# The gate side of the last feed-forward group as seven half products among the output products, with row sums and projections by DMA

## The chip, the cores and the metric

One core of a Trainium2 chip runs the whole program. The metric is the device time of one execution in microseconds (us). Matmuls run on TensorE (PE in the profile, its weight loads PEld), elementwise work on VectorE (DVE), activations and copies out of PSUM on ScalarE (ACT). GpSimd (POOL) issues the accumulating DMAs and SyncE (SP) most of the others. Every engine works through its own instruction queue in order.

## The reference, cut to what matters

The input x has 2048 tokens of 512 features. After a layer norm, two branches are added to x: a state-space layer with 512 complex states, and a gated feed-forward with 1792 hidden features.

```python
xn = layernorm(x)
Bu = xn @ B_bar.T                      # complex, 512 states
h[t] = Lam_bar * h[t-1] + Bu[t]        # over 2048 tokens
A = 2 * real(h @ C.T) + xn * Dskip
gate, up = xn @ w1, xn @ w3            # 512 -> 1792
B = (silu(gate) * up) @ w2             # 1792 -> 512
out = x + A + B                        # bfloat16
```

## The kernel before, in words

**Tiling.** The tokens go in 4 blocks of 512, a block in 4 chunks of 128, two chunks in a *pair*: 8 pairs, 0 to 7, two for each block. Hidden features go in 14 tiles of 128. For each block the normalised input is transposed (`xnT`), projected to the states (`bu`, or `bu_fast` for blocks 2 and 3), multiplied by a table, scanned over time on VectorE (L505) and multiplied by the table again; the feed-forward writes `silu(gate) * up` next to the states in one tile `act`. The output of a pair is one product of `act` with the stacked weights `w2` and C, 22 tiles deep.

**Seven products for eight.** A product of 2 x 2 quarters is made by seven products of quarters and sums of them. The left quarters are a11, a12, a21, a22, with the row sums s1 = a21 + a22, s2 = s1 - a11 (or, in `row_sums`, the same up to the order: s3 = a11 - a21, s2 = s3 - a22), s4 = a12 - s2 or a12 + s2; the right quarters and their sums t1 to t4 likewise. Three things are made so:

- the output of a pair (`y_fast`, L1036): seven products of 11 matmuls, 256 columns wide (`mms`, L1052). Products are numbered 1 to 7; in pairs 4 to 6 their order is 1, 4, 2, 6, 5, 7, 3 (`ORDER`). In pairs 4 and 5 the third product is put off into the next pair, behind its fifth (`LATER`).
- the projection of blocks 2 and 3 (`bu_fast`, L760): half products of 4 matmuls, 256 columns wide. Partial results are copied between PSUM tiles by ScalarE (L785), and two quarters of each half are finished by an addition of PSUM and a saved sum s5 on VectorE (L792).
- the up side of 12 of the 14 hidden tiles of block 3, in three groups n of four tiles (`glu_last`, L838, `product`, L866). The half products come in the order one, five, two, six, seven, three, four. The gate side of the same tiles (`side`, L845) is plain: 4 matmuls of 512 columns for a tile, read by ScalarE's silu (L860).

**Row sums.** `row_sums` (L992) gives for each pair the tasks for s3 and s2 (VectorE subtractions, L1000, 1408 elements for each partition) and s1 (an accumulating DMA from POOL, L1007, or VectorE).

**What sets the order.** The schedule is by hand: instructions stand on each queue in the order in which Python emits them. `bg`, a `Filler` (L23), holds VectorE's background tasks (table products, scans, row sums) with an estimated cost. `bg.fill()` emits tasks while VectorE's estimated time is not too far ahead of TensorE's; `bg.own` books the time of what is emitted directly; `bg.flush(key)` emits all up to a task of that name. A task with a `ready` that says no holds up the queue behind it. `ssm_tasks` (L462) gives the table products (`pre_a`, `pre_b`), their sum (`pre_c`, by VectorE for block 0 and half 0 of block 2, else by DMA), the scans, and the products after the scan (`post_a` to `post_c`). `seeds` (L1013) puts part of the result into four PSUM tiles ahead of a pair.

**The end of the program.** Pairs 2 and 3 run with block 3's projection between their products. Then comes `glu_last(3)`: tiles 12 and 13 plain, then groups 0, 1 and 2. Then pairs 4 and 5 (block 2), 6 and 7 (block 3). VectorE's scans of block 3 run between.

Of the kernel before, what the change touches and what calls it, by code (L numbers as in the profile page):

```python
# [22 lines left out]
class Filler:  # L23
# [25 lines left out]
    def fill(self, lead=None):  # L49
# [14 lines left out]
def kernel(  # L64
# [33 lines left out]
    LEAD = 1.7  # L98
    LATER = (4, 5)
    AHEAD = (MID, 8, 1, None)  # L100
# [361 lines left out]
    def ssm_tasks(b, posts_last=False, between=(), middle=(), late=()):  # L462
# [5 lines left out]
        def half(hf):  # L468
# [3 lines left out]
            def pre_a():  # L472
                if b == 0:
                    sin_step((2 * hf + 1, 1))
                    nc.vector.tensor_scalar(out=tabe[:, psl, 2, :], in0=tabe[:, psl, 1, :], scalar1=-1.0,
                                            scalar2=None, op0=ALU.mult)
                st["g"] = u_blk[b, hf]
# [6 lines left out]
                nc.vector.tensor_tensor(out=st["p"][:, :, ::-1, :], in0=st["g"], in1=tabe[:, psl, 2:0:-1, :],  # L484
                                        op=ALU.mult)

            def pre_b():
                nc.vector.tensor_tensor(out=st["g"], in0=st["g"], in1=tabe[:, psl, 0:1, :].to_broadcast(FULL),  # L488
                                        op=ALU.mult)
# [32 lines left out]
            def post_c(csl=slice(0, CPB)):  # L522
# [3 lines left out]
                else:  # L526
                    gp.dma_start(out=a, in_=p16, accum_op=ALU.add)  # L527

            if (b, hf) == (1, 1):
                pre_c.ready = lambda: ("squares", 2, CPB - 1) in sins_done  # L530
# [5 lines left out]

        transfers = (post0[2],) + (() if b == NBLK - 1 else (post1[2],)) + ((pre1[2],) if b > 0 else ()) + ((pre0[2],) if b in (1, 3) else ())

# [221 lines left out]
    def bu_fast(b, hf):  # L760
# [7 lines left out]
        else:  # L768
            u = up.tile([P, 2, 2, TBLK], BF16, name="u")
        s5 = glup.tile([P, 2, TBLK], BF16, name="g16").bitcast(FP32).rearrange("p a t -> p (a t)")  # L770
        if (b, hf) != (3, 1):
# [17 lines left out]

        def add(out, ps):  # L790
            bg.own(0.7)
            nc.vector.tensor_tensor(out=out, in0=parts(ps), in1=parts(s5), op=ALU.add)  # L792
# [33 lines left out]
    def up_sums(b):  # L826
# [8 lines left out]
                for out, x, z, op in ((s1, a21, a22, ALU.add), (s3, a11, a21, ALU.subtract),  # L835
                                      (s2, s1, a11, ALU.subtract))]

    def glu_last(b):  # L838
        xnT = xnT_blk[b]
# [36 lines left out]

        def add(out, ps):
            bg.own(0.7)
            nc.vector.tensor_tensor(out=out, in0=halves(ps), in1=halves(s5), op=ALU.add)

        gates = []
        for f in range(4 * NG, NFT):
            if f % 2 == 0:
                tiles = pair_tiles()
            gate_side(f, tiles[0])
            copy(tiles[1][:, f % 2, :], side(w3_sb, f))
            bg.fill()
            if f % 2 == 0 and gates:
                gates.pop()()
            if f % 2 == 1:  # L890
                gates.append(lambda f=f, tiles=tiles: gate(f - 1, tiles))
        for n in range(NG):
            f0 = 4 * n
            a11, a12, a22, s1n, s2n, s3n, s4n = (v[:, :, n, :] for v in (
                up_quarter(0, 0), up_quarter(1, 0), up_quarter(1, 1), s1, s2, s3, s4))
            g, e = (ps_y.tile([P, TBLK], FP32, name="y_ps") for _ in range(2))
            f, z = (ps_bu.tile([P, TBLK], FP32, name="bu_ps") for _ in range(2))
            upper, lower = pair_tiles(), pair_tiles()
            product(g, a11, b11, True)
            copy(f, g)  # L900
            product(e, s1n, t1, True)
            copy(s5, e)
            gate_side(f0, upper[0])
            bg.fill(0.8)
            gates.pop()()
            product(f, a12, b21, False)
            product(g, s2n, t2, False)
            copy(e, g)
            bg.own(0.42)
            nc.vector.tensor_tensor(out=s4n, in0=a12, in1=s2n, op=ALU.subtract)  # L910
            copy(upper[1][:, :, 0:TH], halves(f))
            gate_side(f0 + 1, upper[0])
            bg.fill()
            product(g, s3n, t3, False)
            copy(z, g)
            add(lower[1][:, :, TH:TBLK], g)
            product(e, s4n, b22, False)
            add(upper[1][:, :, TH:TBLK], e)
            gate_side(f0 + 2, lower[0])
            bg.fill()  # L920
            gate(f0, upper)
            product(z, a22, t4, False)
            copy(lower[1][:, :, 0:TH], halves(z))
# [4 lines left out]
        return gates.pop()  # L928

# [59 lines left out]

    sums = {}  # L990

    def row_sums(n, b, p):  # L992
# [6 lines left out]
        def subtract(out, x, z):  # L999
            return lambda: nc.vector.tensor_tensor(out=out, in0=x, in1=z, op=ALU.subtract)  # L1000

        three = (0.84, subtract(s3, a11, a21), ("sums", n))
        two = (0.84, subtract(s2, s3, a22), ("sums", n))
        if n in (1, 6, 7):
            one = (0.84, lambda: nc.vector.tensor_tensor(out=a21, in0=a21, in1=a22, op=ALU.add), ("sums", n))
        else:
            one = (0.0, lambda: gp.dma_start(out=a21, in_=a22, accum_op=ALU.add), ("sums", n))  # L1007
        return [three, two, one] if n > 5 else [three, one, two]

# [3 lines left out]
    def seeds(n):  # L1013
        b, p = pairs[n]
        bg.flush(("res", b))
        if n in (0, 3, 5, 7):
# [16 lines left out]
    later = {}  # L1033
    ORDER = {4: (1,4,2,6,5,7,3), 5: (1,4,2,6,5,7,3), 6: (1,4,2,6,5,7,3)}

    def y_fast(n, then=(), between=()):  # L1036
# [4 lines left out]
        bg.flush(("difference", b))  # L1041
        if p == 0 and b > 1:
            bg.flush(("scan", b + 1))
        c1 = 2 * p
        v = sums[n]
        res = xn_blk[b]
        g, halves, f, z = seeded[n]
# [31 lines left out]
        def product1():  # L1079
            mms(g, v["a11"], weight(0, D1), True)  # L1080
            copy(f, g)
            if b > 0:
                bg.first(list(then))
            steps()
            bg.fill()

        def product2():
# [4 lines left out]
            if n in (2, 3, 4, 5):  # L1092
                gp.dma_start(out=v["s4"], in_=v["s2"], accum_op=ALU.add)
            else:
# [5 lines left out]
            if n + 1 < len(pairs) and n not in (1, 2, 3) and n - 1 not in LATER:  # L1100
                seeds(n + 1)
            steps()

        def product3():
# [7 lines left out]
            if b > 0:  # L1112
                steps()
            bg.fill(0.5 if n == 1 else None)

        def product4():
            mms(z, v["a22"], tsum[3], False)
            copy(q[2], z)
            steps()
            bg.fill(1.2 if b > 0 and n not in LATER else None)  # L1120

        def product5():
# [4 lines left out]
            if b > 0:  # L1127
                bg.fill(0.5 if n == 3 else None)

        def product6():  # L1130
            mms(g, v["s2"], tsum[1], False)
            add(q0, g, o1[:, D2].bitcast(FP16))
            steps()
            bg.fill()

        def product7():
# [5 lines left out]
            if b == 0:  # L1142
                steps()
                bg.fill()

        products = (product1, product2, product3, product4, product5, product6, product7)
        for i in ((1, 5, 2, 6, 4, 3, 7) if b == 0 else (1, 2, 4, 6, 5, 7, 3) if b == 1 else ORDER.get(n, (1, 4, 2, 6, 5, 7, 3))):
# [8 lines left out]
            if n in LATER:  # L1156
                bg.fill()
            if between:
                for step in between.popleft():
                    step()  # L1160
                    bg.fill()
                if n == 3 and not between:
                    bg.first(up_sums(3))
            if n == 2 and i == 7:
                seeds(3)

# [74 lines left out]
    bg.flush("up")  # L1241
    gate = glu_last(3)
    gate()
    for n in range(4, len(pairs)):
        ahead = row_sums(n + 1, *pairs[n + 1]) if n + 1 < len(pairs) else ()
# [6 lines left out]
        y_fast(n, ahead if n == 4 else ())  # L1252

# [29 lines left out]
```

## Time and profile before

| | us |
|---|---|
| median of 3 runs | 201.09 (201.04 to 201.39) |
| span of the profiled execution, first to last instruction | 199.5 |
| busy in it: PE | 195.6 |
| DVE | 181.8 |
| ACT | 135.0 |
| POOL | 51.5 |

Of the profiled execution the profile gives the span alone. The runs' median is 1.6 us above it. All times in the profile count from the start of the span. A row of the timeline gives start, length, engine, line, operation, output and input tiles, shape, and in brackets the idle time before it with what ended it; rows of equal instructions are merged, and neighbours on an engine can overlap a little. A row of groups gives count, busy time, mean length in ns, and idle time. A row of waits gives who waited for whom, the total in us, how often, and the longest.

### The profile page before, as it was taken

What the parts mean: (1) busy time and instruction counts of PE and PEld (TensorE: products, weight loads), DVE (VectorE), ACT (ScalarE), POOL (GpSimd) and SP (SyncE); (2) the same over time, 40 slices, a digit from 0 to 9 for tenths busy, and PEclk for the clock granted to TensorE, in tenths of its full rate; (3) what the DMA queues carried; (4) which work ended last, traced back from release to release, by engine and by line L of the source; (5) the groups of instructions that cost most, each with busy time, mean ns of one, the idle gap of its engine ahead of it and who ended that gap; (6) DMA issues with size and microseconds to landing.
All of it is one profiled execution on the core that took longest, in us unless ns stands there. A gap on an engine that the chain in (4) does not pass through costs nothing.

```text
span 199.5 us, 3700 instructions
## 1 busy us (share of the span) xinstructions
PE 195.6 (98%) x1401; PEld 130.7 (65%) x1401; DVE 181.8 (91%) x254; ACT 135.0 (68%) x281; POOL 51.5 (26%) x75
## 2 busy tenths in 40 slices
PE   8999999999999999999999999999999999999994
PEld 2774444444444488866555468888566678888893
DVE  3689699999999999989999997999999999999972
ACT  4699897699999996968998684362588783111220
POOL 7180289700411134041202305040021303310000
PEclk9999999999999999999999999999999999999999
DMA  4999996991497054730997455838137732941111
GB/s 138 326 277 200 302 186 124 343 273 23 69 181 141 0 105 82 135 105 0 156 148 119 89 92 98 172 83 132 53 59 129 149 56 52 174 92 36 53 44 40
DMA packets 32258, 25.12 MB, mean 126 GB/s; under 512 B 16240, under 2 KB 29936, under 8 KB 32240
## 3 DMA queue, kind: packets, MB, share of 16 engines
q0 software_dynamic: 6128, 11.38, 33.5%
q1 hardware_dynamic: 25536, 13.21, 26.8%
q10 hardware_dynamic: 576, 0.30, 0.5%
q8 instruction: 11, 0.18, 0.4%
q14 instruction: 7, 0.06, 0.1%
HBM read 7.74 MB, written 2.10 MB: 49 GB/s over the span
## 4 chain that ended last, share of the span: by engine, by line
PE 95%; DMA 2%; SPq 1%; issue 0%; DVE 0%
PE gu_ps L587 34%; PE gu_ps L1054 17%; PE y_ps L1054 10%; PE gu_ps L848 7%; PE bu_ps L1054 7%; PE bu_ps L454 3%; PE y_ps L454 3%; PE y_ps L869 3%; PE y_ps L780 3%; DMA w_sb<-in_B_w_dram 2%; PE gu_ps L619 2%; PE gu_ps L780 2%; PE bu_ps L869 1%; PE bu_ps L780 1%; PE bu_ps L619 1%; SPq L166 0%
## 5 line engine op out<-in xcount | busy, mean ns | idle before, releaser
L587 PE MATMUL gu_ps<-xnT,w_sb 128*128 128x512 bf16 x312 | 69.6, 379 | 0.0
L587 PEld LDWEIGHTS <-w_sb 128*128 128x128 bf16 x312 | 30.5, 98 | 34.2
L1054 PEld LDWEIGHTS <-act 128*128 128x128 f16 x462 | 43.5, 98 | 5.4
L596 ACT ACTIVATE g<-gu_ps 128x512 bf16<-128x512 f32 x41 | 24.8, 606 | 6.0 <-PE gu_ps L587 3.6
L597 ACT ACTIVATE u<-gu_ps 128x512 bf16<-128x512 f32 x41 | 24.8, 606 | 4.5 <-PE gu_ps L587 3.7
L505 DVE TENSOR_TENSOR_SCAN u<-rho,ends,u 128x512 bf16<-128x512 f32 x16 | 20.0, 1270 | 0.0
L527 POOL DMA_DIRECT2D act<-p x7 | 9.2, 1320 | 34.0 <-DVE act L519 22.1
L1054 PE MATMUL gu_ps<-w_sb,act 128*128 128x256 bf16 (+3 forms) x126 | 16.0, 267 | 0.0
L848 PE MATMUL gu_ps<-xnT,w_sb 128*128 128x512 bf16 x64 | 15.9, 379 | 0.0
L604 DVE TENSOR_TENSOR act<-g,u 128x1024 f16<-128x1024 bf16 x21 | 14.2, 679 | 0.4 <-ACT u L597 0.4
L860 ACT ACTIVATE g<-gu_ps 128x512 bf16<-128x512 f32 x14 | 8.4, 599 | 5.4 <-PE gu_ps L848 5.0
L454 PEld LDWEIGHTS <-bt 128*128 128x128 bf16 x64 | 6.3, 98 | 7.5
L1077 ACT ACTIVATE x_blk<-gu_ps 128x256 f32<-128x256 f32 (+1 forms) x9 | 3.3, 368 | 10.6 <-PE gu_ps L1054 10.6
L1054 PE MATMUL bu_ps<-w_sb,act 128*128 128x256 bf16 (+3 forms) x84 | 10.4, 264 | 0.0
L1054 PE MATMUL gu_ps<-ct,act 128*128 128x256 f16 (+1 forms) x72 | 10.4, 267 | 0.0
L848 PEld LDWEIGHTS <-w_sb 128*128 128x128 bf16 x64 | 6.3, 98 | 4.8
L505 DVE TENSOR_TENSOR_SCAN u<-rho,u 128x512 bf16<-128x512 f32 x8 | 9.2, 1206 | 0.0
L1054 PEld LDWEIGHTS <-x_blk 128*128 128x128 f16 x88 | 8.6, 98 | 1.0
L1054 PEld LDWEIGHTS <-tw 128*128 128x128 f16 x88 | 8.6, 98 | 1.0
L513 DVE TENSOR_TENSOR p<-u,tabe 128x2048 f16<-128x2048 bf16 (+1 forms) x8 | 8.7, 1085 | 0.1
L519 DVE TENSOR_TENSOR act<-u,tabe 128x2048 f16<-128x2048 bf16 (+1 forms) x8 | 8.7, 1083 | 0.0
L488 DVE TENSOR_TENSOR u<-u,tabe 128x2048 bf16<-128x2048 bf16 x7 | 8.5, 1219 | 0.1
(203 smaller groups left out, 392.5 us busy)
## 6 DMA issues: line engine op xcount, KB each, us to landing
act<-p POOLq DMA_DIRECT2D x6, 512.0 KB, 6.1
xn<-x_blk POOLq DMA_DIRECT2D x4, 512.0 KB, 5.5
out_dram<-xn SPq DMA_DIRECT2D x15, 128.0 KB, 1.7
w_sb<-in_B_w_dram SPq DMA_DIRECT2D x1, 1792.0 KB, 8.2
act<-act POOLq DMA_DIRECT2D x5, 352.0 KB, 4.6
w_sb<-in_B_w_dram SPq DMA_DIRECT2D x2, 768.0 KB, 6.4
u<-p POOLq DMA_DIRECT2D x3, 512.0 KB, 5.1
w_sb<-in_B_w_dram SPq DMA_DIRECT2D x4, 256.0 KB, 4.9
```

Of the source, the lines that this page charges most:

```text
L454: nc.tensor.matmul(out=ps, lhsT=bt[:, ri, dt, pt * P:(pt + 1) * P], rhs=xnT_blk[b][:, dt, :], start=(dt == 0), stop=(dt == NDT - 1))
L505: nc.vector.tensor_tensor_scan(out=v, data0=rho[:, pt:pt + 1].to_broadcast([P, TBLK]), data1=v, initial=init, op0=ALU.mult, op1=ALU.add)
L513: nc.vector.tensor_tensor(out=by_state(st["p16"][:, csl]), in0=by_chunk(st["g"][:, :, ::-1, tsl]), in1=by_chunk(tabe[:, psl, 2:0:-1, tsl]) ...
L519: nc.vector.tensor_tensor(out=by_state(act_state(b, hf)[:, csl]), in0=by_chunk(st["g"][:, :, :, tsl]), in1=by_chunk(tabe[:, psl, 0:1, tsl] ...
L527: gp.dma_start(out=a, in_=p16, accum_op=ALU.add)
L587: nc.tensor.matmul(out=ps[:, tsl], lhsT=w[:, dt, f * P:(f + 1) * P], rhs=xnT[:, dt, tsl], start=(dt == 0), stop=(dt == NDT - 1))
L596: nc.scalar.activation(out=g16[:, f % 2, :], in_=g_ps, func=ACT.Silu)
L597: nc.scalar.activation(out=u16[:, f % 2, :], in_=u_ps, func=ACT.Copy)
L604: nc.vector.tensor_tensor(out=act_gates(b, f - 1), in0=split(g16), in1=split(u16), op=ALU.mult)
L780: nc.tensor.matmul(out=out[:, h * TH:(h + 1) * TH], lhsT=left[:, h, k, :], rhs=right[:, k, :], start=(start and h == 0 and k == 0), stop=( ...
L848: nc.tensor.matmul(out=ps, lhsT=w[:, dt, f * P:(f + 1) * P], rhs=xnT[:, dt, :], start=(dt == 0), stop=(dt == NDT - 1))
L1054: nc.tensor.matmul(out=out, lhsT=left[:, k, :], rhs=right[k][:, cols], start=(start and k == 0), stop=(k == NK - 1), skip_group_check=True)
```

## The change

1. **Gate side of group 2 by half products.** The four plain gate sides of the third group become seven half products. Their row sums (`gate_sums`) are made by VectorE in the slots of the up sums of groups 0 and 1 that are no longer needed, and in place in `w1`. Where the up side adds into an SBUF tile, the gate side adds in PSUM and then takes the silu.
2. **Third group beside pair 4.** Its up products one and five stay ahead of pair 4; the other twelve steps go in between pair 4's products, after product 1: two and six; after 4: seven, three; after 2: four (`last`), and the gate's one and five; after 6: two, six; after 5: seven, three; after 7: four and a gate multiplication; after 3: the last gate multiplication. Pair 4's third product is no longer put off (`LATER` holds 5 alone); pair 5's seeds use other PSUM tiles, and come after pair 4's product 7.
3. **VectorE's queue in pairs 4 and 5.** `bg.fill` does nothing there; after each product a fixed number of tasks is emitted (`PACE`, `Filler.take`).
4. **Row sums by DMA.** s3 of pair 4, and s3 and s2 of pair 5, are a ScalarE copy with scale -1, in one piece (pair 4) or two (768 and 640 elements, pair 5), and an accumulating DMA from POOL.
5. **Projection of block 3 by DMA.** The two additions of each half become a ScalarE copy and an accumulating DMA of fp16.
6. **Block 2, half 0:** `pre_c` becomes an accumulating DMA; its `post_c` is held until pair 3 has issued its s4.

```diff
+    def take(self, n):
+        for _ in range(min(n, len(self.tasks))):
+            self.pop()
...
-    LATER = (4, 5)
+    LATER = (5,)
...
             def pre_c():
-                if b == 0 or (b, hf) == (2, 0):
+                if b == 0:
...
+            if (b, hf) == (2, 0):
+                post_c.ready = lambda: 3 in taken
...
         def add(out, ps):
+            if by_dma:
+                copy(out, parts(ps))
+                gp.dma_start(out=out, in_=parts(s5), accum_op=ALU.add)
+                return
...
+    def gate_sums():
+        s1, s2 = (ups["s"][i][:, :, 0, :] for i in range(2))
+        a11, a12, a21, a22 = (gate_quarter(*i) for i in ((0, 0), (1, 0), (0, 1), (1, 1)))
+        s3 = gate_quarter(0, 1, True)
+        u2 = ups["s"][1][:, :, NG - 1, :]
+        u4, s4 = (ups["s"][i][:, :, 1, :] for i in range(2))
...
+            def end(out, ps):
+                nc.scalar.activation(out=out, in_=halves(ps), func=ACT.Silu if gated else ACT.Copy)
+            def add(out, ps):
+                bg.own(0.7)
+                nc.vector.tensor_tensor(out=halves(ps) if gated else out, in0=halves(ps), in1=halves(s5), op=ALU.add)
+                if gated:
+                    end(out, ps)
...
-        for n in range(NG):
+        for n in range(NG - 1):
...
             copy(s5, e)
+            by_copy[5][0][n + 1]()
...
+        return (one, five, by_copy[5][1][1], first), deque(((two, six, by_copy[5][1][2]), (seven, three), (last, gone, gfive), (gtwo, gsix),
+                                          (gseven, gthree), (glast, lambda: gate(f0, upper)), (lambda: gate(f0 + 2, lower),)))
...
+        def from_copy(out, x, z, k0, k1, transfer):
+            nc.scalar.activation(out=out[:, k0:k1], in_=z[:, k0:k1], func=ACT.Copy, scale=-1.0)
+            if transfer:
+                gp.dma_start(out=out, in_=x, accum_op=ALU.add)
...
+    PACE = {4: {1: 0, 4: 1, 2: 2, 6: 2, 5: 1, 7: 2, 3: 0}, 5: {1: 1, 4: 0, 2: 0, 6: 3, 5: 2, 7: 0, 3: 0}}
...
+            if n in PACE:
+                bg.take(PACE[n][i])
+                if (n, i) == (4, 7):
+                    bg.flush(("scan", 3))
+                    sums_by_dma(5)
```

The first `add` with `by_dma` is that of `bu_fast`, where `by_dma` is true for block 3; `end` and the second `add` belong to a new function `group` in `glu_last`, called once for the up side and once, with `gated`, for the gate side. `one` to `seven` and `last` are the half products' steps; `gone` to `glast` are those of the gate side. In the sum s2 of the gate side the sources are the same as for the up side, and `by_copy[4][0][0]`, pair 4's copy, stands ahead of tile 12.

More of the change, by code (lines that the diff above doesn't have):

```diff
@@ L891, in glu_last @@
                 gates.append(lambda f=f, tiles=tiles: gate(f - 1, tiles))
-        for n in range(NG):
+        for n in range(NG - 1):
             f0 = 4 * n
[L894 to L897, printed above, removed]
+            lefts = up_lefts(n)
             upper, lower = pair_tiles(), pair_tiles()
[L899 to L902, printed above, removed]
+            one, five, two, six, seven, three, last = group(
+                lefts, lambda: sums4(lefts[6], lefts[1], lefts[4]), upper[1], lower[1], False)
+            one()
+            five()
+            by_copy[5][0][n + 1]()
             gate_side(f0, upper[0])
@@ L905, in glu_last @@
             gates.pop()()
[L906 to L911, printed above, removed]
+            two()
+            six()
             gate_side(f0 + 1, upper[0])
             bg.fill()
[L914 to L918, printed above, removed]
+            seven()
+            three()
             gate_side(f0 + 2, lower[0])
@@ L921, in glu_last @@
             gate(f0, upper)
-            product(z, a22, t4, False)
-            copy(lower[1][:, :, 0:TH], halves(z))
+            last()
             gate_side(f0 + 3, lower[0])
@@ L1007, in row_sums, with third @@
             one = (0.0, lambda: gp.dma_start(out=a21, in_=a22, accum_op=ALU.add), ("sums", n))
+        if n in ():
+            def third():
+                nc.scalar.activation(out=s3, in_=a22, func=ACT.Copy)
+                gp.dma_start(out=s3, in_=s2, accum_op=ALU.add)
+            by_copy[n] = third
+            return [one, (0.84, subtract(s2, a11, a21), ("sums", n))]
         return [three, two, one] if n > 5 else [three, one, two]
@@ L1099, in product2 @@
                 store(c1, o1, D1)
-            if n + 1 < len(pairs) and n not in (1, 2, 3) and n - 1 not in LATER:
+            if n + 1 < len(pairs) and n not in (1, 2, 3, 4) and n - 1 not in LATER:
                 seeds(n + 1)
@@ L1119, in product4 @@
             steps()
-            bg.fill(1.2 if b > 0 and n not in LATER else None)
+            fill(1.2 if b > 0 and n not in LATER else None)
         def product5():
@@ L1241 @@
     bg.flush("up")
-    gate = glu_last(3)
-    gate()
+    sums5 = row_sums(5, *pairs[5])
+    begin, beside = glu_last(3)
+    for step in begin:
+        step()
+    bg.take(2)
     for n in range(4, len(pairs)):
-        ahead = row_sums(n + 1, *pairs[n + 1]) if n + 1 < len(pairs) else ()
+        ahead = (sums5 if n == 4 else row_sums(n + 1, *pairs[n + 1])) if n + 1 < len(pairs) else ()
         if n > 4:
```

131 lines of the change are left out of this document (109 added, 22 removed).

## The prediction

> **What bounds the kernel now.** I read the page's busy times, then its chain of work that ended last, then the waits of TensorE alone, then TensorE's timeline.
>
> ```profile
> PE 195.6 (98%) x1401; PEld 130.7 (65%) x1401; DVE 181.8 (91%) x254; ACT 135.0 (68%) x281; POOL 51.5 (26%) x75
> ...
> PE 95%; DMA 2%; SPq 1%; issue 0%; DVE 0%
> ```
>
> TensorE is busy for 195.6 of 199.5 us and makes 95% of the chain. Its waits:
>
> ```profile
> PE bu_ps L196 <- PEq L1267: 0.8, 1, 0.8
> PE gu_ps L619 <- DMA w_sb<-in_B_w_dram: 0.3, 1, 0.3
> PE y_ps L243 <- DVE xn L224: 0.2, 1, 0.2
> ```
>
> All three lie in the start-up. From then on only fewer matmuls can gain anything; a wait that is new on TensorE is paid in full, and an engine that is merely lightened gives nothing. TensorE's timeline, with the last block's feed-forward (L848 full sides, L869 half products) and the output products (L1054):
>
> ```profile
> 139.88 3.62 PE L848 MATMUL gu_ps<-xnT,w_sb 128*128 128x512 bf16 x16
> 143.34 0.60 PE L869 MATMUL y_ps<-xnT,w_sb 128*128 128x256 bf16 x4
> ...
> 146.83 0.60 PE L869 MATMUL y_ps<-x_blk,w_sb 128*128 128x256 f16 x4
> ...
> 156.40 0.60 PE L869 MATMUL y_ps<-xnT,w_sb 128*128 128x256 bf16 x4
> 156.83 0.60 PE L869 MATMUL y_ps<-x_blk,bt 128*128 128x256 f16 x4
> ...
> 177.34 1.36 PE L1054 MATMUL y_ps<-tw 128*128 128x256 f16 x11
> 178.54 0.93 PE L1054 MATMUL gu_ps<-w_sb,act 128*128 128x256 bf16 x7
> ```
>
> From start to start, a 512-wide matmul takes (143.34 - 139.88)/16 = 0.216 us, a half product of four 0.435 (0.109 a matmul), an output product 1.20. A half product's result is there 0.60 after its start, 0.17 after its successor's.
>
> **Part 1, the saving.** The third group's gate side goes from 4 full sides (16 matmuls) to 7 half products (28). 16 x 0.216 = 3.46; 28 x 0.109 = 3.05. TensorE loses 0.41 us. Nothing else is added to it or taken from it: the group's up side only moves in between pair 4's products, and pair 4's late third product goes back into place.
>
> [...]
>
> **Part 2, ScalarE's three copies.** The row sums of pairs 4 and 5 become a copy by -1 on ScalarE and an accumulating DMA: one copy of 1408 columns ahead of the last block, one of 768 + 640 in its first two groups, one of 768 + 640 among pair 4's first products. No row has such a width; the nearest:
>
> ```profile
> L290 ACT ACTIVATE xn<-x_blk,acc,rstd_all 128x512 bf16<-128x512 bf16 x8 | 6.1, 805 | 1.6 <-POOL acc L285 1.6
> ...
> L274 ACT ACTIVATE xn<-x_blk 128x512 bf16<-128x512 bf16 x4 | 2.5, 621 | 0.0
> ```
>
> and ScalarE's queue in the first group (columns: start, length):
>
> ```profile
> 144.03 0.59 ACT L857 ACTIVATE bu_ps<-y_ps 128x512 f32<-128x512 f32 x1
> 144.55 0.59 ACT L857 ACTIVATE bt<-y_ps 128x512 f32<-128x512 f32 x1
> ...
> 146.19 0.58 ACT L857 ACTIVATE y_ps<-y_ps 128x512 f32<-128x512 f32 x1 [0.32 <-PE y_ps L869]
> 146.69 0.59 ACT L857 ACTIVATE u<-bu_ps 128x512 bf16<-128x512 f32 x1
> 147.17 0.60 ACT L860 ACTIVATE g<-gu_ps 128x512 bf16<-128x512 f32 x1
> 147.64 0.62 ACT L857 ACTIVATE bu_ps<-y_ps 128x512 f32<-128x512 f32 x1
> ```
>
> and in pair 4:
>
> ```profile
> 156.60 0.60 ACT L860 ACTIVATE g<-gu_ps 128x512 bf16<-128x512 f32 x1 [0.21 <-PE gu_ps L848]
> ...
> 163.63 0.38 ACT L1028 ACTIVATE gu_ps<-xn 128x256 f32<-128x256 bf16 x1
> 163.93 0.38 ACT L1030 ACTIVATE gu_ps<-xn 128x256 f32<-128x256 bf16 x1
> ```
>
> 512 columns take 0.60, 256 take 0.38: 256 more cost 0.22. L274 is a plain copy within SBUF like the new ones, so 768 columns take 0.62 + 0.22 = 0.84, 640 take 0.73, 1408 take 1.39. Below: 0.59 + 0.22 = 0.81. Above: L290's 0.805 gives 1.03 and 0.92. I take L274, the same operation. Neighbours in the queue overlap by 0.11 (0.60 long, 0.49 apart), so the pieces hold the queue for 0.73 and 0.62.
>
> *First group.* The copy at 146.19 ends at 146.77, and the product at 146.83 reads what it has freed: it is already the last to arrive. Now the 768 columns stand behind 144.55: from 145.05 to 145.78, then the silu to 146.27, then that copy, 0.08 late. **TensorE waits 0.08 us.** In the second group the piece is 0.11 shorter: about 0.
>
> *Pair 4.* Without a wait TensorE starts, in the new order, u1 at 156.40, u5 156.83, P1 157.27, u2 158.47, u6 158.91, P4 159.35, u7 160.55, u3 160.98, P2 161.42, u4 162.62, then the gate side's g1 163.06, g5 163.49, P6 163.93, g2 165.13, g6 165.57, P5 166.00, g7 167.20, g3 167.64, P7 168.08, g4 169.28, P3 169.71, pair 5 170.91 with its seventh product at 176.91, pair 6 178.11 (u and g: the half products of the up and gate side; P: pair 4's). ScalarE does the silu at 156.60, two seeds to 157.69, two copies (0.52, 0.50) to 158.71, 768 columns to 159.44, P1's copy to 159.75, u6's copy until 160.33 (u7 needs it by 160.55: in time), u2's way out from 160.24, 640 columns from 160.73 to 161.35, P4's copy to 161.65, u7's copy until 162.25. u7 was done at 161.15: the row sum makes its copy 0.5 late. Behind that stand VectorE's two additions:
>
> ```profile
> 148.29 1.29 DVE L879 TENSOR_TENSOR u<-y_ps,bt 128x512 bf16<-128x512 f32 x2 [0.38 <-ACT bu_ps L857]
> ```
>
> They begin 0.03 after the copy that they wait for (147.64 + 0.62), so they run here from 162.28 to 163.57. g1 needs the first (done at 162.97, before 163.06), g5 the second: 163.57 and 0.06 to notice it is 163.63, for 163.49. **TensorE waits 0.14 us.**
>
> *The 1408 columns* wait for block 3's first state accumulation:
>
> ```profile
> 132.93 1.41 POOL L527 DMA_DIRECT2D act<-p  x1
> ```
>
> ```profile
> DMA to landing us min/median/max: 6.3/6.3/6.3
> ```
>
> It lands at 139.2, and 1.4 us more is 140.6, ahead of the last block's first silu (the first 512-wide sum is done at 139.88 + 0.86 + 0.17 = 140.9). Cost 0. If it lands later, ScalarE's queue moves, and the copy of 146.19 pays.
>
> **Part 3, VectorE** loses one 2048-wide addition, four projection additions and three row sums, and gains four gate sums and two additions for the gate side in place in PSUM. TensorE was not waiting for it, so the relief is worth 0. No row shows an addition that writes PSUM: 0.60 like L879 (1.29 for two, less the overlap), not less, for its operands are the same; at most twice that, for a second pass through PSUM. I take 0.60. The one close date is pair 5's addition after its sixth product, which must be done by 176.91. From g7's start, 167.20: product 0.60, 0.07, copy 0.62, 0.03, that is 168.52. Then, by
>
> ```profile
> 162.84 0.69 DVE L864 TENSOR_TENSOR act<-g,u 128x1024 f16<-128x1024 bf16 x1
> 163.45 1.28 DVE L505 TENSOR_TENSOR_SCAN u<-rho,act,u 128x512 bf16<-128x512 f32 x1
> ...
> 170.41 0.69 DVE L1139 TENSOR_TENSOR xn<-gu_ps,x_blk 128x512 bf16<-128x512 f32 x1
> 171.02 3.63 DVE L505 TENSOR_TENSOR_SCAN x_blk<-rho,act,x_blk 128x512 bf16<-128x512 f32 x3
> 174.56 0.40 DVE L1065 TENSOR_TENSOR xn<-bu_ps,xn 128x256 bf16<-128x256 f32 x1
> ...
> 183.55 0.42 DVE L1065 TENSOR_TENSOR q<-gu_ps,xn 128x256 f32<-128x256 f32 x1
> 183.89 0.68 DVE L513 TENSOR_TENSOR p<-u,tabe 128x1024 f16<-128x1024 bf16 x1
> 184.49 0.68 DVE L519 TENSOR_TENSOR act<-u,tabe 128x1024 f16<-128x1024 bf16 x1
> ```
>
> two additions 1.20, three scans 3.55, one output of 512 0.61, two gate multiplications 1.21, one p 0.60, three 256-wide additions 0.34 + 0.34 + 0.42: 8.27, to 176.79, and 0.06 to notice it. The margin is 0.06 us against errors of about as much over twelve instructions: I put **0.03 us**.
>
> **Part 4, POOL and the transfers.** Eight more; the nearest rows:
>
> ```profile
> act<-p POOLq DMA_DIRECT2D x6, 512.0 KB, 6.1
> ...
> act<-act POOLq DMA_DIRECT2D x5, 352.0 KB, 4.6
> ```
>
> The projections' last one is issued before pair 3 ends at 139.88, landed at the latest at 146.0 and read when VectorE comes to it, after 146; pair 4's row sum is issued at 140.6, landed by 147 and read after u6 of the second group, at 153; pair 5's are issued behind ScalarE's pieces at 152.2 and 161.4 and due at 174.5. POOL's queue holds nothing behind them that is due sooner. Cost 0; without that cover, VectorE's queue is late by what the transfer is late.
>
> **Sum.** -0.41 + 0.08 + 0.14 + 0.03 = -0.16 us on the span of 199.5. The median of 201.09 lies 1.6 above that span, which the change leaves alone: **200.93 us.**
>
> **The rivals.** A measurement of this kernel tells apart about 0.2%, 0.40 us, so even the whole saving barely shows.
>
> - *Nothing waits*: 201.09 - 0.41 = 200.68. For it: every wait that I found is within 0.15 us of its date, which a little more overlap removes. Chance 0.25.
> - *ScalarE's copies decide, slower.* The place is the queue ahead of u6's copy in the first group and u7's in pair 4. Every 0.1 us more on each piece costs 0.1 there and 0.2 here. The saving is gone from 0.05 more on a piece (0.16/3). At L290's price, 0.19 more on each, 0.57 is added: 201.5; in proportion to width (1.21 for 768, 1.01 for 640) 0.37 and 0.28 more give 1.02: 201.95. Against it: L290 has two per-partition operands, the new copies none. Chance 0.16.
> - *VectorE is late for pair 5's seventh product.* It decides from 0.06 us on; with the two PSUM additions at twice 0.60 it is 1.2 later: 202.1. For it: VectorE is full from g7 on. Chance 0.08.
> - *A transfer lands late*, the state accumulation ahead of the 1408 columns above all: landed after 139.6 it makes ScalarE's first silu late, after about 140.8 TensorE too, one for one; 3 us later than before gives 1.4 more, 202.3. For it: new transfers share its queues. Chance 0.06.
> - *Narrow matmuls cost more than their columns*, since weight loads go from 16 to 28:
>
> ```profile
> L848 PEld LDWEIGHTS <-w_sb 128*128 128x128 bf16 x64 | 6.3, 98 | 4.8
> ```
>
> If these twelve at 98 ns were not hidden, 1.18 us would be added and the sum would be +1.02: 202.1. The 0.109 of the rows, with a load for each matmul, all but excludes it. Chance 0.01. [...]
>
> **How the numbers follow.** Forecast 0.44, with its own range 200.75 to 201.15. Faster by over 0.2% needs less than 200.69: the first rival and a little of the forecast's low end, 0.27. Slower, over 201.49: most of the second rival and parts of the next three, 0.25. Within: 0.48. The range, 200.55 to 201.7, reaches from the first rival less 0.13 of spread between runs to past the second rival's price at L290; outside are the dearer halves of the second and third rivals and the latest transfers, under 0.2.
>
> **What would show it.** Right: 1413 matmuls, pair 6 beginning 0.1 to 0.3 us earlier, TensorE waiting for ScalarE's copy in the first group and for VectorE's addition at g5, pieces of 0.84 and 0.73. Wrong: a wait of TensorE over 0.3 us anywhere, above all ahead of pair 5's seventh product; pieces over 0.95; or no wait at all.

## The result, and the profile after

The changed kernel takes **200.64 us** (median; 200.49 to 200.92) beside 201.18 for the kernel before on the same chip: a ratio of 0.9973, 95% interval 0.9963 to 0.9984. Run once more in another job it took 200.84 beside 201.12: 0.9982, 0.9967 to 0.9997. The forecast was 200.93 with a range of 200.55 to 201.7; both medians lie inside it, on the side that was forecast, and the first of them lies near its low end. The profiled execution after took 200.49 us, with a span of 198.7.

The page of after, its busy times and the share of each engine in the chain that ended last:

```profile
PE 194.5 (98%) x1400; PEld 132.4 (67%) x1413; DVE 178.4 (90%) x252; ACT 142.6 (72%) x294; POOL 60.2 (30%) x83
...
PE 98%; issue 0%; DVE 0%
```

and the only row of its waits of TensorE:

```profile
PE bu_ps L200 <- PEq L1410: 0.8, 1, 0.8
```

Twelve weight loads more (1413; of the matmuls 13 records are missing in this profile, a second one of the same kernel has x1413 for them and 195.3 us of busy time), VectorE lighter by 3.4 us, ScalarE heavier by 7.6, POOL by 8.7; TensorE still bounds everything. No wait outside the start-up is listed; what TensorE waits in the stretch that the change touches is under 0.1 us at a place, and has to be read from the starts in its timeline. First the two ends of that stretch (L594 is the first wide matmul of the whole program, L883 that of the last block, the last row is pair 6's first):

```profile
12.38 8.80 PE L594 MATMUL gu_ps<-xnT,w_sb 128*128 128x512 bf16 x39
...
139.38 2.97 PE L883 MATMUL gu_ps<-xnT,w_sb 128*128 128x512 bf16 x12
...
145.44 1.03 PE L883 MATMUL gu_ps<-xnT,w_sb 128*128 128x512 bf16 x4
146.39 0.60 PE L904 MATMUL y_ps<-x_blk,w_sb 128*128 128x256 f16 x4
...
158.90 1.36 PE L1186 MATMUL gu_ps<-tw,act 128*128 128x256 f16 x11
160.10 0.60 PE L904 MATMUL y_ps<-x_blk,w_sb 128*128 128x256 f16 x4
...
162.62 0.60 PE L904 MATMUL y_ps<-xnT,w_sb 128*128 128x256 bf16 x4
163.10 0.60 PE L904 MATMUL y_ps<-x_blk,bt 128*128 128x256 f16 x4
...
175.32 0.93 PE L1186 MATMUL y_ps<-w_sb,act 128*128 128x256 f16 x7
...
176.53 1.36 PE L1186 MATMUL bu_ps<-tw 128*128 128x256 f16 x11
177.73 0.93 PE L1186 MATMUL gu_ps<-w_sb,act 128*128 128x256 bf16 x7
```

In the profiled execution of before the first of these stood here, and the other two at 139.88 and 178.54:

```profile
12.88 8.80 PE L587 MATMUL gu_ps<-xnT,w_sb 128*128 128x512 bf16 x40
```

Three lengths tell where the 0.8 us between the two spans lie. From the first wide matmul to the last block both take 127.00. From pair 6 to the end of the span before takes 20.96 and after 20.97. **From the last block to pair 6 it is 38.66 before and 38.35 after: the change is worth 0.31 us.** The other 0.50 is the start-up, which the change leaves alone; a second profile of the kernel before starts early too, and has the same 127.00 and 38.66:

```profile
12.35 8.80 PE L587 MATMUL gu_ps<-xnT,w_sb 128*128 128x512 bf16 x39
...
139.35 2.97 PE L848 MATMUL gu_ps<-xnT,w_sb 128*128 128x512 bf16 x12
...
178.01 0.93 PE L1054 MATMUL gu_ps<-w_sb,act 128*128 128x256 bf16 x7
```

The 0.31 come apart as follows. The narrower products give 0.41 (16 x 0.216 less 28 x 0.109, as forecast). In the first group (tiles 0 to 3) the product at 146.39 comes 0.95 after the four 512-wide matmuls at 145.44, which take 0.87: TensorE waits 0.08. Before it was 0.88 at the same place (145.95 to 146.83), so 0.07 are lost. The gate side's second half product g5 (163.10) comes 0.48 after its first, g1 (162.62), which takes 0.435: 0.05 lost. The third group's u7 (160.10) follows its predecessor (158.90) after that one's 1.20, without the 0.02 that it lost before; pair 5's seventh product comes 1.21 after the sixth, which is no loss. -0.41 + 0.07 + 0.05 - 0.02 = -0.31.

ScalarE's rows of after, with the new copies (L1105) and what stands behind them:

```profile
138.99 1.38 ACT L1105 ACTIVATE x_blk<-act 128x1408 f16<-128x1408 f16 x1 [1.16 <-DMA act<-p]
140.44 0.60 ACT L895 ACTIVATE g<-gu_ps 128x512 bf16<-128x512 f32 x1
...
144.52 0.84 ACT L1105 ACTIVATE tw<-act 128x768 f16<-128x768 f16 x1
...
145.73 0.61 ACT L892 ACTIVATE y_ps<-y_ps 128x512 f32<-128x512 f32 x1
...
157.26 0.56 ACT L892 ACTIVATE bu_ps<-y_ps 128x512 f32<-128x512 f32 x1
157.74 0.60 ACT L892 ACTIVATE bt<-y_ps 128x512 f32<-128x512 f32 x1
158.22 0.85 ACT L1105 ACTIVATE tw<-act 128x768 f16<-128x768 f16 x1
...
160.20 0.76 ACT L1105 ACTIVATE tw<-act 128x640 f16<-128x640 f16 x1
160.83 0.41 ACT L1209 ACTIVATE x_blk<-gu_ps 128x256 f32<-128x256 f32 x1
161.09 0.64 ACT L892 ACTIVATE bu_ps<-y_ps 128x512 f32<-128x512 f32 x1
```

The copy at 145.73 ends at 146.34, and the product at 146.39 adds into the tile that this copy reads, so it has to wait for it. The copy at 161.09 ends at 161.73, and VectorE's two additions begin 0.03 later. VectorE's rows of after: the up side's additions into SBUF, the gate side's into PSUM, and the addition that pair 5's seventh product waits for:

```profile
161.76 1.29 DVE L922 TENSOR_TENSOR u<-y_ps,bt 128x512 bf16<-128x512 f32 x2 [0.66 <-ACT bu_ps L892]
...
168.06 1.30 DVE L922 TENSOR_TENSOR y_ps<-y_ps,bt 128x512 f32<-128x512 f32 x2 [0.78 <-ACT bu_ps L892]
...
175.86 0.41 DVE L1197 TENSOR_TENSOR x_blk<-bu_ps,xn 128x256 f32<-128x256 f32 x1
```

### The profile page after: what moved, and what is told of

Same layout as the page of the kernel before. It is cut to its first block, busy times and chain, and to the rows that moved or that the text cites. A ratio compares the mean times of both kernels' runs of the same rounds, so it can differ in the third digit from the quotient of the medians.

```text
span 198.7 us, 3744 instructions
## 1 busy us (share of the span) xinstructions
PE 194.5 (98%) x1400; PEld 132.4 (67%) x1413; DVE 178.4 (90%) x252; ACT 142.6 (72%) x294; POOL 60.2 (30%) x83
## 4 chain that ended last, share of the span: by engine, by line
PE 98%; issue 0%; DVE 0%
PE gu_ps L594 34%; PE gu_ps L1186 18%; PE y_ps L1186 9%; PE bu_ps L1186 7%; PE gu_ps L883 5%; PE y_ps L904 4%; PE y_ps L458 3%; PE bu_ps L458 3%; PE y_ps L792 3%; PE bu_ps L200 2%; PE gu_ps L626 2%; PE bu_ps L904 2%; PE gu_ps L792 2%; PE bu_ps L792 1%; PE bu_ps L626 1%; PE y_ps L247 1%
## 5 line engine op out<-in xcount | busy, mean ns | idle before, releaser
L594 PE MATMUL gu_ps<-xnT,w_sb 128*128 128x512 bf16 x304 | 68.9, 379 | 0.4
L594 PEld LDWEIGHTS <-w_sb 128*128 128x128 bf16 x312 | 30.5, 98 | 34.2
L603 ACT ACTIVATE g<-gu_ps 128x512 bf16<-128x512 f32 x41 | 24.8, 606 | 6.2 <-PE gu_ps L594 3.3
L532 POOL DMA_DIRECT2D act<-p x7 | 9.9, 1407 | 23.3 <-DVE act L524 23.1
L883 PE MATMUL gu_ps<-xnT,w_sb 128*128 128x512 bf16 x45 | 11.5, 379 | 0.1
L1186 PE MATMUL bu_ps<-w_sb,act 128*128 128x256 bf16 (+3 forms) x77 | 9.5, 263 | 0.0
L904 PEld LDWEIGHTS <-w_sb 128*128 128x128 bf16 (+1 forms) x72 | 7.0, 98 | 2.8 <-issue 0.2
L493 DVE TENSOR_TENSOR u<-u,tabe 128x2048 bf16<-128x2048 bf16 (+1 forms) x7 | 8.6, 1222 | 0.1
L1186 PE MATMUL gu_ps<-tw,x_blk 128*128 128x256 f16 x66 | 8.2, 272 | 0.0
L223 DVE BATCH_NORM_STATS2 stats<-x_blk 128x6 f32<-128x512 bf16 x8 | 5.4, 676 | 2.9 <-DMA x_blk<-in_A_x_dram 2.9
```

The lines of the kernel that those rows point to most:

```text
L594: nc.tensor.matmul(out=ps[:, tsl], lhsT=w[:, dt, f * P:(f + 1) * P], rhs=xnT[:, dt, tsl], start=(dt == 0), stop=(dt == NDT - 1))
L603: nc.scalar.activation(out=g16[:, f % 2, :], in_=g_ps, func=ACT.Silu)
L883: nc.tensor.matmul(out=ps, lhsT=w[:, dt, f * P:(f + 1) * P], rhs=xnT[:, dt, :], start=(dt == 0), stop=(dt == NDT - 1))
L904: nc.tensor.matmul(out=out[:, h * TH:(h + 1) * TH], lhsT=left[:, k, h * P:(h + 1) * P], rhs=right[:, k, :], start=(start and h == 0 and k ...
L1186: nc.tensor.matmul(out=out, lhsT=left[:, k, :], rhs=right[k][:, cols], start=(start and k == 0), stop=(k == NK - 1), skip_group_check=True)
```

## The experiments

**The theory:** the half products are the whole gain, 0.41 us; the ScalarE copies give a little of it back in the first group and at g5; all else in the change only makes room. **The rivals:** the relief of VectorE, the DMAs or the paced queue quicken something themselves; or the 0.54 us measured first hold a second gain. Below, *distance* is the time from the last block's first matmul to pair 6's first, in the profiled execution: 38.66 before, 38.35 changed. The ratios are to the kernel before, run in the same job.

| kernel | ratio (95% interval) | distance |
|---|---|---|
| before, once more | 1.0007 (0.9997 to 1.0017) | 38.66 |
| changed | 0.9973 (0.9963 to 0.9984) | 38.35 |
| changed, once more | 0.9982 (0.9967 to 0.9997) | 38.35 |
| gate side plain | 1.0004 (0.9995 to 1.0012) | 38.70 |
| first groups' copies later | 0.9984 (0.9973 to 0.9994) | 38.28 |
| all pieces later | 0.9982 (0.9971 to 0.9993) | 38.24 |
| all pieces later, once more | 0.9983 (0.9971 to 0.9994) | 38.24 |
| pieces twice | 1.0131 (1.0097 to 1.0165) | 41.57 |
| pair 5's sums on VectorE | 1.0215 (1.0153 to 1.0277) | 43.43 |
| projection on VectorE | 1.0083 (1.0054 to 1.0113) | 38.35 |
| block 2's sum on VectorE | 0.9989 (0.9973 to 1.0006) | 38.35 |
| queue not paced | 0.9974 (0.9964 to 0.9985) | 38.35 |

### The kernel before, and the changed one, once more

No edit. They give the spread between executions.

> The kernel before against itself: what the comparison gives for no change. Both theories: within 0.2% of 1. If the first block's start in this profile lies 0.3 us or more from the 12.88 us of the first profile, the changed kernel's 12.38 is the start-up's own spread, and of the 0.54 us measured only the 0.31 behind the last block's start belongs to the change.

> The changed kernel once more, beside the next two. Theory (the half products are the whole gain): the distance from the last block's first matmul to pair 6 is 38.35 us again, against 38.66 before, wherever the start-up falls; time 0.3 us (0.15%) under before, 200.7 to 200.85, so the 0.54 us seen first is 0.3 and a favourable draw. Rival (the change also quickens something else, worth another 0.2): 0.5 us under before again.

Before took 201.05 us beside 201.06. The changed kernel took 200.84 beside 201.12: 0.28 us, close to its 0.31 of distance and to what was expected. The draw of 0.54 was the favourable one; a second gain is not seen in the trace: both profiles have the same 38.35, and the same lengths ahead of the stretch and behind it. The intervals alone would not decide it; the two overlap for gains from 0.32 to 0.66 us.

### The gate side plain again

The third group's gate side is four full sides of four 512-wide matmuls between pair 4's products; the up side and the order stay as changed. Most of the gate's row sums and its two additions on VectorE fall away with the half products (VectorE is busy for 176.2 us instead of 178.4).

```diff
...
-        gone, gfive, gtwo, gsix, gseven, gthree, glast = (gate_step(i) for i in range(7))
...
+        plain = [lambda i=i, p=p: gate_side(f0 + i, (upper, lower)[i // 2][0], p) for i, p in enumerate((y, y, bu_, bu_))]
...
-(last, gone, gfive), (gtwo, gsix), (gseven, gthree), (glast, lambda: gate(f0, upper)),
+(last, plain[0]), (plain[1],), (plain[2],), (plain[3], lambda: gate(f0, upper)),
```

> The changed kernel with the third group's gate side plain again, four sides of four 512-wide matmuls among pair 4's products; row sums and projections by DMA, pacing and order as changed. Theory 1: 0.41 us more on TensorE, and the same waits or fewer: distance 38.70 to 38.76, time 201.0 to 201.1, level with the kernel before. Theory 2: the gain stays, 38.3 to 38.4, 200.6 to 200.7.

201.09 us beside 201.06: with all the relief for VectorE, the DMAs and the pacing, but without the half products, nothing is gained. The timeline of TensorE, with two of the full sides:

```profile
139.54 2.75 PE L883 MATMUL gu_ps<-xnT,w_sb 128*128 128x512 bf16 x11
...
166.90 1.03 PE L883 MATMUL bu_ps<-xnT,w_sb 128*128 128x512 bf16 x4
167.76 1.36 PE L1184 MATMUL gu_ps<-tw,x_blk 128*128 128x256 f16 x11
...
178.24 0.93 PE L1184 MATMUL gu_ps<-w_sb,act 128*128 128x256 bf16 x7
```

A full side takes 0.86 (166.90 to 167.76), as in before. The distance is 0.35 longer than with the half products: 0.41, less the 0.05 that g5 loses. Against the kernel before it is 0.04 longer, about the 0.07 lost in the first group less the 0.02 at u7. So the new place of the third group, with all that makes room for it, gains nothing by itself.

### The copies of pair 5's row sums later

First, the 768 + 640 columns of the first two groups go from behind the fifth half product to behind the third; second, the pieces in pair 4 move back by a step each as well.

```diff
             five()
-            by_copy[5][0][n + 1]()
...
             three()
+            by_copy[5][0][n + 1]()
...
-(one, five, by_copy[5][1][1], first), deque(((two, six, by_copy[5][1][2]), (seven, three), (last, gone, gfive),
+(one, five, first), deque(((two, six), (seven, three, by_copy[5][1][1]), (last, gone, gfive, by_copy[5][1][2]),
```

> The piece of the row-sum copy in the first two groups moves behind the half product three, into ScalarE's idle 0.50 us. Distance meant below: from the last block's first 512-wide matmul to pair 6's first matmul; 38.66 us before, 38.35 after the change. Theory 1 (the gain is TensorE's 0.41 less the waits that are left, 0.08 in the first group and 0.05 ahead of g5): the wait of 0.08 goes, distance 38.27, time 0.08 us under the changed kernel's. Theory 2 (the gain comes from VectorE's relief, and the waits on ScalarE do not reach the end): distance and time unchanged, 38.35.

> As before, and pair 4's two pieces too move to where ScalarE is idle, behind u7's copy and behind g5's. Theory 1: u7's copy starts 0.35 us earlier, both waits go, distance 38.22 us (38.66 less 0.41, less 0.02 that the kernel before already waits in each of two groups), time 0.12 under the changed kernel's. Theory 2: 38.35.

> Both moves of the row-sum copies, beside the changed kernel on one chip. Theory: the distance is 38.24 again, 0.11 us under the changed kernel's, as no matmul waits in the first group or at g5; the times differ by 0.1 us, too little for an interval to part. Rival (the moves cost something later on that the profile of one execution missed): slower than the changed kernel by 0.2 us or more.

TensorE's timeline with all pieces later:

```profile
139.75 2.54 PE L883 MATMUL gu_ps<-xnT,w_sb 128*128 128x512 bf16 x10
...
145.82 1.03 PE L883 MATMUL gu_ps<-xnT,w_sb 128*128 128x512 bf16 x4
146.70 0.60 PE L904 MATMUL y_ps<-x_blk,w_sb 128*128 128x256 f16 x4
...
162.93 0.60 PE L904 MATMUL y_ps<-xnT,w_sb 128*128 128x256 bf16 x4
163.37 0.60 PE L904 MATMUL y_ps<-x_blk,bt 128*128 128x256 f16 x4
...
177.99 0.93 PE L1186 MATMUL gu_ps<-w_sb,act 128*128 128x256 bf16 x7
```

The product of 146.70 comes 0.88 after its predecessor (0.95 in after) and g5 0.44 after g1 (0.48): both waits are gone, down to the 0.02 that the first group loses in the kernel before too. Moving the first groups' copies alone shortens the distance by 0.07, moving pair 4's as well by 0.04 more. So the two losses are shown to be the copies' doing, one for each place. In time (200.89, 200.65 and 200.78 us, beside 201.06, 201.06 and 201.12) a tenth of a microsecond can't be seen; by distance this is the best of the kernels here, 0.11 us ahead of the changed one.

### The pieces twice

Each of pair 5's four copies is executed twice.

```diff
-            nc.scalar.activation(out=out[:, k0:k1], in_=z[:, k0:k1], func=ACT.Copy, scale=-1.0)
+            for _ in range(2 if n == 5 else 1):
+                nc.scalar.activation(out=out[:, k0:k1], in_=z[:, k0:k1], func=ACT.Copy, scale=-1.0)
```

> Each ScalarE piece of pair 5's row sums is done twice (the second writes the same again): 0.73 us more queue in the first group and 0.62 in the second, 0.73 and 0.62 in pair 4. Theory 1 (ScalarE's queue is at its limit at these places): waits of 0.81 in the first group, about 0.55 in the second, and 1.35 to 1.4 in all ahead of u7, g1 and g5; distance 38.35 + 2.6 = 40.9 to 41.0, time 203.2. Rival (ScalarE, 72% busy, has room): distance under 38.6.

203.96 us, and TensorE now waits for long enough to be listed; its waits, beyond the start-up:

```profile
PE y_ps L904 <- ACT y_ps L892: 1.8, 3, 0.8
...
PE bu_ps L904 <- ACT bu_ps L892: 0.4, 1, 0.4
```

The starts in the timeline put what is lost in three places: first group 0.96 (0.88 more than in after), second group 0.73 (0.71 more), pair 4 1.69 (1.65 more, ahead of u7, u4, g1 and g5). Together that is 3.2 us, the whole difference in distance. It is about 0.6 more than expected, because the expectation took each repeat to overlap its neighbour by 0.11 us, as other neighbours in the queue do. A copy and its repeat don't overlap (1.71 for the two, where one took 0.84 in after):

```profile
144.90 1.71 ACT L1106 ACTIVATE tw<-act 128x768 f16<-128x768 f16 x2
```

From here to the start of the silu behind it are 1.62 us (144.90 to 146.52), and 0.73 in after (144.52 to 145.25): the repeat moves the queue by 0.89, and not by 0.73. Read in the same way, the queue moves by 0.79 in the second group and by 1.68 in pair 4, so nearly each microsecond of ScalarE at these places is a microsecond of TensorE. It is the slope that the forecast's rival of dearer copies used, for the first group and pair 4; the second group, which that rival left out, has it too once some 0.08 us of slack are used up.

### Pair 5's row sums back on VectorE

s3 and s2 of pair 5 are subtractions again, at the end of pair 4; no pieces on ScalarE.

```diff
-            by_copy[5][0][n + 1]()
...
-        if n in (4, 5):
+        if n in (4,):
             three = (0.0, lambda: None, ("sums", n))
-        if n == 5:
+        if n in ():
             two = (0.0, lambda: None, ("sums", n))
```

> Pair 5's two row sums s3 and s2 back on VectorE (0.80 us each, behind the scans at pair 4's end), no ScalarE pieces and no transfers for them; the rest as changed. Theory 1: both waits on ScalarE go (0.13 less), but the sums stand in VectorE's queue ahead of pair 5's sixth product, which reads s2: done about 1.6 us late, distance 38.2 + 1.4 to 1.7 = 39.6 to 39.9, 201.9 to 202.2 in all. Rival (VectorE's relief is worth nothing, as TensorE was not waiting for it before): distance 38.2.

205.33 us (204.56 to 207.22), three more than expected. TensorE's timeline in pair 5:

```profile
173.90 0.60 PE L1185 MATMUL bu_ps<-ct,act 128*128 128x256 f16 x4
176.07 1.37 PE L1185 MATMUL bu_ps<-tw 128*128 128x256 f16 x11 [1.57 <-DVE tw L1101]
179.27 1.04 PE L1185 MATMUL y_ps<-w_sb,act 128*128 128x256 f16 x4 [1.82 <-DMA act<-act]
...
183.13 0.93 PE L1185 MATMUL gu_ps<-w_sb,act 128*128 128x256 bf16 x7
```

The first wait was expected: VectorE comes to the two subtractions only behind two scans,

```profile
171.85 2.46 DVE L510 TENSOR_TENSOR_SCAN x_blk<-rho,act,x_blk 128x512 bf16<-128x512 f32 x2
174.22 0.87 DVE L1101 TENSOR_TENSOR tw<-act 128x1408 f16<-128x1408 f16 x1
175.13 0.89 DVE L1101 TENSOR_TENSOR tw<-tw,act 128x1408 f16<-128x1408 f16 x1
```

(The brackets count from the modelled end of the matmul before, some 0.17 late; from its duration the two waits are 1.73 and 2.00.) The second wait was not expected. s1 is added by DMA on top of a21, which s3 still has to read; so its transfer, issued at 166.76 in the changed kernel, starts behind the first subtraction, 3.9 us before TensorE can go on:

```profile
175.39 0.91 POOL L1121 DMA_DIRECT2D act<-act  x1 [8.28 <-DVE tw L1101]
```

Nor was what followed. The windows of 1 us from the second wait on (the columns are the length, the busy time and count of PE, PEld, DVE, ACT and POOL, and then TensorE's granted clock, the DMA share and GB/s):

```profile
178.00:179.00 1.00, 0.00 (x0) 0.00 (x0) 0.97 (x3) 0.00 (x0) 0.00 (x0) 0.93 1.04 218
179.00:180.00 1.00, 0.73 (x4) 0.55 (x5) 1.00 (x2) 0.00 (x0) 0.00 (x0) 0.50 1.02 206
...
181.00:182.00 1.00, 1.00 (x6) 0.71 (x5) 1.00 (x2) 0.17 (x1) 0.00 (x0) 0.50 0.04 3
182.00:183.00 1.00, 1.00 (x10) 0.85 (x8) 0.07 (x1) 0.21 (x1) 0.00 (x0) 0.86 0.00 0
```

The clock falls to half just before TensorE starts again (a mean of 0.93 in the window from 178 to 179), and by the windows' means stays there for some 0.1 + 3 + 0.3 = 3.4 us. From 173.90 to 183.13 TensorE takes 9.23 us where after's rows give 0.435 + 3 x 1.20 = 4.04: 1.73 for the first wait, 2.00 for the second, 1.46 for the slow clock. These 5.19, less the 0.11 that the missing pieces no longer cost in the first group and at g5, are the 5.08 by which the distance is longer. The slow clock is not in every execution: of the four, the profiled one (205.89 us) has a mean granted clock of 0.992 and the slowest (207.22) 0.983, but 204.56 and 204.78 us came with 1.000. The two waits alone are 3.73. The row-sum copies are thus no gain of their own; they are what the new place of the third group costs, since at this point of its queue VectorE has no room for these sums. Whether another place in the queue has room for them was not tried.

### The projection, and block 2's sum, back on VectorE

```diff
-                st["g"] = st["v"].bitcast(BF16) if b in (3,) else st["v"]
+                st["g"] = st["v"]
...
-        by_dma = b in (3,)
+        by_dma = b in ()
```

> Block 3's projection additions back on VectorE (four at 0.60 us), the rest as changed. Theory 1: VectorE, which in the changed order also carries half 1's products ahead of the last block, comes 2.4 us later to the first group's s4 (done at 146.60, needed by 146.82): TensorE waits about 2 us there, distance 40.2 to 40.6, 202.4 to 202.9. Rival (relief worth nothing): 38.35.

```diff
-                if b == 0:
+                if b == 0 or (b, hf) == (2, 0):
                     nc.vector.tensor_tensor(out=st["g"], in0=st["g"], in1=st["p"], op=ALU.add)
```

> Block 2's first pre_c back on VectorE (1.14 us at about 107 us), the rest as changed. Theory 1: VectorE idles for 1 us and more before the last block in the changed kernel, so this addition costs nothing by then: distance 38.35, time as changed. Rival (the changed order needs it): 0.3 to 1.1 us more.

With the projection's additions on VectorE the distance is 38.35, unchanged: the wait of 2 us that was expected in the first group does not come. What is put back on VectorE surfaces only behind the stretch, in the last pairs, where TensorE waits for the table products (L530) and for a row sum (L1102):

```profile
PE y_ps L1186 <- DVE act L530: 0.9, 2, 0.6
...
PE gu_ps L1186 <- DVE x_blk L1102: 0.3, 1, 0.3
```

It takes 203.01 us; from pair 6 to the end of the span it takes 22.8 instead of 21.0. The expectation thus had the place wrong, and the rival, for which this relief is worth nothing, has the time wrong. Block 2's sum alone costs nothing that can be seen (201.06 beside 201.11, distance 38.35), as expected.

### The queue not paced

```diff
-        fill = (lambda *lead: None) if n in PACE else bg.fill
+        fill = bg.fill
...
-                bg.take(PACE[n][i])
```

> VectorE's queue in pairs 4 and 5 filled by the planner's estimates and not by fixed numbers; nothing else differs. The gate side's two additions then stand behind two scans more and one less later. Theory (dates on VectorE have slack here): they come 0.4 us later, at 168.5, and still in time for pair 5's seeds; the addition ahead of pair 5's seventh product is done about 176.1, in time: distance 38.35, time as changed. Rival (the pacing is what makes the change possible, since its margins are under 0.1 us): a wait of TensorE in pair 5 of 0.4 us or more, time 0.4 to 1.2 us above changed.

200.70 us, distance 38.35. VectorE's rows, in an execution that starts 0.42 later than after's:

```profile
168.94 1.27 DVE L922 TENSOR_TENSOR y_ps<-y_ps,bt 128x512 f32<-128x512 f32 x2
...
176.28 0.42 DVE L1197 TENSOR_TENSOR x_blk<-bu_ps,xn 128x256 f32<-128x256 f32 x1
```

The gate side's additions come 0.46 later than in after (168.94 - 0.42 - 168.06), yet pair 5's addition is done at 176.70, a quarter of a microsecond ahead of its product at 176.95. The fixed numbers gain nothing over the planner here.

## Why the prediction was right

**The saving** (part 1): -0.41 as forecast, shown by the plain gate side (0.35, with g5's loss gone too). The rival of narrow matmuls that cost more is out: four narrow ones took 0.435 throughout. The 128-wide matmuls at the end of the program cost little more than their columns too: seven of them take 0.39 from start to start (192.14 to 192.53 in after), 56 ns each, and a quarter of the 512-wide one's 216 ns is 54.

**The copies** (part 2): 0.84, 0.73 and 1.39 forecast from L274; 0.84 to 0.85, 0.73 to 0.76 and 1.38 measured. The rival at L290's price falls with that. In the first group the forecast wait of 0.08 was there to the hundredth (0.07 of it new, as the kernel before waits there too). **At g5 the term was mis-sized: 0.14 forecast, 0.05 measured.** The mechanism is the one named (u7's late copy, then VectorE's second addition), but the chain to it was added up too slowly. ScalarE's two copies ahead of the 768 columns follow each other by 0.48, not 0.52 and 0.50, and pair 4's copy after the 640 columns holds the queue for 0.26, not 0.30; u7's copy ends 0.08 sooner than the sum has it, counted from u1. The copy of 1408 columns cost nothing, as forecast, but with less to spare: it began 0.3 later than the sum has it, counted from the last block's start, as its transfer took 6.7 us to land and not 6.3, and it ended at 140.37, 0.07 ahead of the silu behind it.

**VectorE** (part 3): additions into PSUM take as long as those into SBUF (1.30 and 1.29 for two), so the upper bound (twice that) is out. Pair 5's seventh product, put at 0.03, lost nothing: the addition ended at 176.27, 0.26 ahead, of which 0.06 go to noticing it (as from 146.77 to 146.83 in before). Counted from g7, VectorE's twelve instructions started 0.07 sooner than summed, and their length was 0.06 shorter. That the relief is worth nothing was right as a gain and wrong as a statement about the change: with the third group in its new place the relief is needed. Where it is missing the profiles show 1.9 us more (projection, in the last pairs) or 5.1 (pair 5's sums, of which 1.46 are the slow clock). Block 2's sum could have stayed on VectorE; pair 4's s3 was not tried.

**The DMAs** (part 4) cost nothing in the changed kernel. In the experiment that held s1's transfer back, it became a wait of 2.00 us on its own.

**The sum.** -0.16 forecast for the stretch, -0.31 measured: 0.09 from g5, 0.03 from the seventh product, some 0.03 from two places, the first group and u7, where the kernel before already lost 0.02 each, which the sum did not set off. So the mechanism held and the size was half of what came. Of the 0.54 us measured first, the other 0.23 are about what two medians of the changed kernel differ by here (200.64 and 200.84); they are not located. The first median, 200.64, lies below the forecast's own 200.75 to 201.15, and the number nearest to it is that of the rival in which nothing waits, 200.68; but the waits are there, at the two places that were named, and go when the copies are moved. That its number came so near is the draw: the second median, 200.84, lies in the forecast's own range. By the distance the gain is 0.31 us (0.15%), within 0.2%; by the times the first run gives 0.27% and the second 0.14%. Of the signs that were named, the 1413 matmuls, the two places and the pieces' lengths came as said, and pair 6 begins 0.31 earlier, at the upper end of 0.1 to 0.3.

## What to carry to other kernels

In this kernel, where TensorE is busy without a gap, the saving in matmul columns arrived in full, and it was the small waits that the change makes on the other queues that had to be summed, instruction by instruction: 0.1 of 0.4 us, and movable. Before work is moved between VectorE's instructions, ask what VectorE has no room for afterwards, and how late that would surface; an edit that gains nothing alone can be what makes the gain possible. To judge a gain below the spread of the start-up, compare the distance between two matmuls on either side of the change, which repeated to 0.01 us, and not the spans.

## What the hardware showed unexpectedly

**The clock fell after two short waits.** After two waits of 1.73 and 2.00 us with 1.20 us of matmuls between them, TensorE's clock was at half for 3.4 us (pair 5's sums on VectorE, the profiled execution). In two of that kernel's four executions the mean clock was 1.000, so these waits don't bring the fall each time; what decides is not shown. The four waits of the kernel with the pieces twice, 0.4 to 0.8 us each, and the three of the projection's, up to 0.6, left the mean clock at 1.000 in all four executions of each.

**The start-up alone spreads by 0.9 us.** In thirteen profiled executions of kernels with the same code there, the first wide matmul starts between 12.35 and 13.24 us. Once, with all pieces later, the unchanged middle also took 127.39 instead of 127.00, in two pauses of about 0.2 us at 75.5 and 80.5 that no view attributes.
